# Top-k attention followed by two feed-forward layers on one core: value loads on 128 partitions, last rows of two batches moved to a later stage, DMA issues planned with slack, small operations on GpSimd

## The chip, the cores and the metric

One core of a Trainium2 chip runs the whole program. The metric is the device time of one execution in microseconds (us). The engines are TensorE (PE; its weight loads are shown apart as PEld), VectorE (DVE), ScalarE (ACT), GpSimd (POOL) and SyncE (SP), which here only issues DMA transfers. Each engine takes its instructions in the order in which the program lists them: an instruction that waits holds up everything behind it on its engine.

## What is computed

Attention over 4 batches, 8 heads, 576 rows and head dimension 64, in which each row keeps its 32 largest scores; then two feed-forward layers (512 to 2048 to 512) over all 2304 rows, one with a leaky maximum and one with a clipped square. All in float32.

```python
scores = scale * np.matmul(q, k.transpose(0, 1, 3, 2))
kth = np.partition(scores, -32, axis=-1)[..., -32:-31]
scores = np.where(scores >= kth, scores, -1e9)
scores = scores - scores.max(axis=-1, keepdims=True)
attn = np.exp(scores)
attn = attn / (attn.sum(axis=-1, keepdims=True) + 1e-09)
x = np.matmul(attn, v)                     # heads joined: 2304 rows x 512
h = x @ moe_w_in;   x = np.maximum(0.01 * h, h) @ moe_w_out
h = x @ moe2_w_in;  g = where(h >= 1, h, where(h <= -1, 0, (h + 1) ** 2 / 4))
out = g @ moe2_w_out
```

## The kernel before

The program does not list its instructions in a fixed order. It states operations with an engine, an estimated duration, the tiles that they read and write and a priority (`Plan.op`, L81), and a planner (`Plan.run`, L112) plays them through: each engine takes the ready operation of the lowest priority number. The order in which it starts them is the order in which they are emitted. The constants at the top (`T_NORM`, `HOP`, `LAT`) and the durations given with each operation steer this order; they put no instruction into the program by themselves. A buffer of a tag comes free `HOP` after its last use, and a dependent operation is ready `LAT` after the one it needs (L204 to L220).

Attention is cut into units. A main unit `("m", b, a, h)` takes 256 rows of one head (two tiles of 128 rows). The 64 rows that are left of the 576 in each head are taken by units `("r", b, 0, h)`, one tile for two heads. `units` (L641) lists them by batch; `REMS` (L31) says in which batch's stage the r units of which batches stand: before, those of batches 0 and 1 stand in batch 1's stage, 8 of them, one of each after every second head. An r unit of the batch that is at work uses the K and V that are loaded; an r unit of another batch loads and splits K and V anew (`kv_new`, L473, called at L666).

A unit goes through these steps:
- `kv_new` and `q_new` load K, V and Q with DMAs on SP and split K and Q into a rounded part (ACT) and a rest (POOL, `sub`, L350). For batches 0 and 1 (`lean_of`) V is loaded doubled as `vl`, for batches 2 and 3 as `vraw` and then split into `vv`. V lies in blocks of `KB` = 116 rows, so its loads go to 116 partitions (L482, L486).
- `scores` multiplies on PE into two banks, and ACT copies them to the tile `s`.
- `topk` finds the 32 largest on DVE: four rounds of a maximum of eight (L533) with three replacements (L537) between them. For the first 72 units ACT then makes a mask by a steep slope (L553) and the exponential (L555); their biases are in `nb`, made by a small ACT operation for the unit (L546) and one for each tile (L549). The sums get 1e-9 added on ACT (L568, tile `rc`), DVE takes the reciprocal (L569), POOL scales the rows (L571).
- Two units later `pv` transposes on PE, copies on ACT (`ptr`), for batches 2 and 3 splits into `pt` on ACT and POOL, multiplies by V, and `gather` puts the result into `xraw` (m) or `xr` (r).

When all units of a block of 256 rows are through, `split_x` makes the input of the first feed-forward layer, and `FLOW` (L34) lets the layers run: the two blocks of batch 0 one after the other through layer 0, together through layer 1, then batch 1 through both layers, batch 2, and at last batch 3 together with the block `"r"` of all remaining rows. Feed-forward work has priority numbers from 10000 on: PE takes it where no attention work is ready. The weights are prepared once for each layer (`prep_w`, L402: two ACT and two DVE operations, a split, and a store to scratch memory) while attention of batches 0 and 1 runs; later they are loaded again from scratch into six `ring` buffers.

Of the kernel before, what the change touches and what calls it, by code (L numbers as in the profile page):

```python
# [27 lines left out]
PREP = (0.7, 4.5, 0.05, 14, 14.0, 0.25)  # L28
HOP = 180
JOINT = (1, 2, 3)  # L30
REMS = {1: (0, 1), 2: (2,), 3: (3,)}  # L31
LATE = ("pt", "xb", "vv")
PREPS = ("wraw", "wa", "wb")
FLOW = [  # L34
    ([((0, 0),)], 0),
# [8 lines left out]
]  # L44
LAG = 2
AHEAD = 2
T_NORM = 750
COLD = 100e3
NLEAN = 16
SOFT = (72, 24)  # L50
# [16 lines left out]
class Plan:  # L67
# [44 lines left out]
    def run(self):  # L112
        n = len(self.ops)
        left = [len(o[4]) for o in self.ops]
        succ = [[] for _ in range(n)]
        for i, o in enumerate(self.ops):
            for d in o[4]:
                succ[d].append(i)
        uses = {}
        for o in self.ops:  # L120
            for ref in o[6]:
                uses[ref] = uses.get(ref, 0) + 1
        given = {}
        slots = {t: {i: 0.0 for i in range(c)} for t, c in self.bufs.items()}

        def slot(ref):

            if ref.fifo and given.get(ref.fifo, 0) != ref.seq:
                return None
            free = slots[ref.tag]  # L130
            can = [i for i in (ref.among or free) if free.get(i, 1e18) <= now]
            return min(can, key=free.get) if can else None

        ready_at = [0.0] * n
        ready = {}
        events = []
        busy = {}
        dma_free = 0.0
        order = []
        for i in range(n):  # L140
            if not left[i]:
                ready.setdefault(self.ops[i][0], []).append((self.ops[i][3], i))
        now, cnt = 0.0, 0
        for q in ready.values():
            q.sort()

        def start(i):
            nonlocal dma_free, cnt
            eng, ns, fn, prio, deps, new, refs = self.ops[i]
            for ref in new:  # L150
                ref.slot = slot(ref)
                del slots[ref.tag][ref.slot]
                given[ref.fifo] = given.get(ref.fifo, 0) + 1
            order.append((now, i))
            if eng == "SP":
                busy[eng] = now + 500.0
                t0 = max(now + 1200.0, dma_free)
                dma_free = t0 + ns
                end = dma_free + 900.0
                heapq.heappush(events, (now + 500.0, cnt, -1))  # L160
                cnt += 1
            else:
                if eng == "PE" and now < COLD:
                    ns *= 1.9
                busy[eng] = now + ns
                end = now + ns
                heapq.heappush(events, (end, cnt, -1))
                cnt += 1
            heapq.heappush(events, (end, cnt, i))
            cnt += 1  # L170

        def pick(eng):
            q = ready.get(eng)
            if not q:
                return None
            for k, (prio, i) in enumerate(q):
                ok = ready_at[i] <= now
                if ok:
                    new = self.ops[i][5]
                    ok = all(slot(r) is not None for r in new) and all(  # L180
                        r.slot is not None or r.tag not in self.bufs or r in new for r in self.ops[i][6]
                    )
                if ok:
                    del q[k]
                    return i
            return None

        done = 0
        while done < n:
            for eng in list(ready):  # L190
                while busy.get(eng, 0.0) <= now:
                    i = pick(eng)
                    if i is None:
                        break
                    start(i)
            if not events:
                raise RuntimeError("no instruction can go on")
            now = max(now, events[0][0])
            while events and events[0][0] <= now:
                _, _, i = heapq.heappop(events)  # L200
                if i < 0:
                    continue
                done += 1
                eng = self.ops[i][0]  # L204
                for ref in self.ops[i][6]:
                    uses[ref] -= 1
                    if uses[ref] == 0 and ref.tag in self.bufs:
                        slots[ref.tag][ref.slot] = now + HOP
                        heapq.heappush(events, (now + HOP, cnt, -1))
                        cnt += 1  # L210
                for j in succ[i]:
                    left[j] -= 1
                    e2 = self.ops[j][0]
                    lat = LAT.get((eng, e2), HOP)
                    ready_at[j] = max(ready_at[j], now + lat)
                    if not left[j]:
                        bisect.insort(ready.setdefault(e2, []), (self.ops[j][3], j))
                        if ready_at[j] > now:
                            heapq.heappush(events, (ready_at[j], cnt, -1))
                            cnt += 1  # L220
        self.span, self.order = now, order
        for _, i in order:
            self.ops[i][2]()


LAT = {("PE", "A"): 200, ("PE", "V"): 200, ("A", "PE"): 230, ("A", "V"): 142, ("A", "P"): 160, ("V", "A"): 128,
       ("V", "PE"): 230, ("V", "P"): 155, ("P", "A"): 75, ("P", "V"): 34, ("P", "PE"): 203, ("SP", "SP"): 300,
       ("A", "A"): 140, ("V", "V"): 127, ("P", "P"): 100, ("PE", "PE"): 0}
# [23 lines left out]
def kernel(  # L252
# [111 lines left out]

    idt = fixed([128, 128], F32, "idt")
    half = fixed([128, 1], F32, "half")
    tiny = fixed([128, 1], F32, "tiny")
    gate = fixed([1, 1], F32, "gate")

    def constants():  # L370
# [31 lines left out]
    def prep_w(key, j):  # L402
# [4 lines left out]
        if (L, i, c) not in raws:  # L407
# [7 lines left out]
        va = bank(among=(2, 3)) if L == 0 else new("wa", [128, DM])  # L415
        bits = new("wb", [128, DM], I32)
        n = DM
        act(va, lambda: raw()[:, z * 2 * n:(z + 1) * 2 * n].bitcast(F32)[:, 1::2], t_a(n), [va], [raw], pr,
            scale=2.0 ** -112)
        act(bits, lambda: raw()[:, z * 2 * n:(z + 1) * 2 * n].bitcast(U16)[:, 1::4], t_a(n), [bits], [raw], pr,  # L420
            scale=2.0 ** -13, bias=-0.49994)
        for shift, op in ((3, ALU.logical_shift_left), (-(2 ** 31), ALU.bitwise_and)):
            vec(lambda shift=shift, op=op: nc.vector.scalar_tensor_tensor(
                out=bits(), in0=va().bitcast(I32), scalar=shift, in1=bits(), op0=op, op1=ALU.bitwise_or),
                t_v(n), [bits], [va, bits], pr)
        if key in pinned:
            wt = fixed([128, 2, DM], F32R, f"pin{L}_{f}_{c}")
            pin_t[key] = wt
# [44 lines left out]
    def kv_new(b, h, pr):  # L473
# [5 lines left out]
        sub(lambda: kk()[D:2 * D], lambda: raw()[D:2 * D], lambda: kk()[D:2 * D], S, [kk], [raw, kk], pr)  # L479
        if lean_of(b, h):  # L480
            vt = new("vl", [128, NJ, 2 * D])
            dma(lambda: vt()[0:KB], lambda: vd[b, h], 290, [vt], [], pr)  # L482
            return kk, vt
        vt = new("vv", [128, NJ, 2 * D], F32R)
        vraw = new("vraw", [128, NJ, D])
        dma(lambda: vraw()[0:KB], lambda: vm[b, h], 145, [vraw], [], pr)  # L486
        ve = h % 2
        split(lambda a: vt()[0:KB, :, (ve if a == 0 else 1 - ve) * D:(ve if a == 0 else 1 - ve) * D + D],
              lambda: vraw()[0:KB], NJ * D, vt, [vraw, gate], 0, pr)
# [34 lines left out]
    def topk(tiles, soft, pr):  # L524
# [19 lines left out]
        if soft:  # L544

            P.op("A", 100, lambda: nc.scalar.mul(out=nb()[:, 0:n, 0:2], in_=m()[:, 0:n, 0:32:31], mul=-scale),  # L546
                 w=[nb], r=[(m, (i, r)) for i in range(n) for r in (0, 3)], prio=pr)
            for i in range(n):
                act(lambda i=i: nb()[:, i, 2:3], lambda i=i: m()[:, i, 31:32], 95, [(nb, (i, 2))],  # L549
                    [(m, (i, 3)), nb], pr, func=ACTF.Identity, scale=scale, bias=lambda i=i: nb()[:, i, 0:1])  # L550
            for i in range(n):

                slope(es[i], tiles[i], 670, STEEP, [es[i]], [tiles[i], nb], pr,  # L553
                      scale=scale, bias=lambda i=i: nb()[:, i, 1:2])
                P.op("A", 763, lambda i=i: nc.scalar.activation(  # L555
                    out=es[i](), in_=es[i](), func=ACTF.Exp, bias=nb()[:, i, 2:3], accum_out=sums()[:, i:i + 1]),
                    w=[es[i], (sums, i)], r=[es[i], (nb, (i, 2))], prio=pr)
        else:
            P.op("A", 100, lambda: nc.scalar.mul(out=nb()[:, 0:n, 0], in_=m()[:, 0:n, 0], mul=-scale),
                 w=[nb], r=[(m, (i, 0)) for i in range(n)], prio=pr)  # L560
            for i in range(n):
# [3 lines left out]
                    out=es[i](), in0=tiles[i](), scalar=m()[:, i, 31:32], in1=es[i](),  # L565
                    op0=ALU.is_ge, op1=ALU.mult, accum_out=sums()[:, i:i + 1]),
                    900, [es[i], (sums, i)], [tiles[i], (m, (i, 3)), es[i]], pr)
        act(lambda: rc()[:, 0:n], lambda: sums()[:, 0:n], 95, [rc], [sums, tiny], pr, func=ACTF.Identity, bias=tiny)  # L568
        vec(lambda: nc.vector.reciprocal(out=rc()[:, 0:n], in_=rc()[:, 0:n]), 70, [rc], [rc], pr)  # L569
        for i in range(n):  # L570
            P.op("P", T_NORM, lambda i=i: nc.gpsimd.tensor_scalar(  # L571
# [164 lines left out]
    class Rows:  # L736
# [11 lines left out]
        def hidden(self, i, ws):  # L748
# [21 lines left out]
            else:  # L770
# [1 line left out]
                t = new("t", [128, 512])  # L772
                vec(lambda: nc.vector.tensor_scalar(out=t(), in0=ps(), scalar1=-1.0, scalar2=1.0, op0=ALU.max, op1=ALU.min),  # L773
                    602, [t], [ps], hi)
                act(t, t, 520, [t], [t, half], hi, func=ACTF.Square, scale=0.5, bias=half)
                vec(lambda: nc.vector.tensor_tensor(out=gr(), in0=ps(), in1=t(), op=ALU.max), 602, [gr], [ps, t], hi)
                act(lambda: gt()[:, 0], gr, t_a(512), [(gt, (0, 0))], [gr], hi)
            sub(lambda: gt()[:, 1], gr, lambda: gt()[:, 0], 512, [(gt, (0, 1))], [gr, (gt, (0, 0))], hi)
# [124 lines left out]
def laid_out(inputs):  # L903
# [20 lines left out]
    nj = -(-S // KB)  # L924
    vp = np.zeros((B, H, nj * KB, D), v.dtype)
    vp[:, :, :S] = v
    vm = vp.reshape(B, H, nj, KB, D).transpose(0, 1, 3, 2, 4)
    data.append(("vm", vm))
    data.append(("vd", np.concatenate([vm, vm], axis=4)))
    for n in _INS[3:]:  # L930
# [29 lines left out]
```

## Time and profile before

| | us |
|---|---|
| median of 3 runs | 1308.94 (1304.5 to 1309.97) |
| the profiled execution, its device time | 1310.76 |
| the profiled execution, its span from first to last instruction | 1308.9 |
| PE busy in it | 1187.5 (91%) |
| DVE busy | 918.3 (70%) |
| ACT busy | 904.4 (69%) |
| POOL busy | 704.2 (54%) |
| mean granted TensorE clock | 0.964 of full speed |

The profiled execution's time is 1.9 us over its span, and 1.8 us over the median of the runs. Matmuls are pipelined and their ends are modelled, so a busy PE is not a PE at its peak. A wait for several semaphores is put down to the one that came last by the profile.

### The profile page before, as it was taken

To read this page: it belongs to the slowest core of one execution; us is meant where nothing else is said; L and a number is where in the kernel's file an instruction comes from. 1 tells how busy PE (TensorE), PEld (TensorE's weight loads), DVE (VectorE), ACT (ScalarE), POOL (GpSimd) and SP (SyncE) were. 2 spreads that over 40 slices of the span, in tenths; PEclk is the share of its full clock that TensorE was granted. 3 is DMA by queue.
4 is the path that set the end of the run, shared out by engine and by line. 5 is a ranking of instruction groups with operands and counts; after the bars stand their busy time and mean duration, and the time that the engine had idled before them with its cause. 6 is when DMAs were issued, how large, how long until landed. Compare 5 with 4: busy or idle time off the path is not lost. (4 is left out here: it accounts for less than half of the span.)

```text
span 1308.9 us, 19465 instructions
## 1 busy us (share of the span) xinstructions
PE 1187.5 (91%) x6448; PEld 1003.4 (77%) x6448; DVE 918.3 (70%) x1822; ACT 904.4 (69%) x2171; POOL 704.2 (54%) x684
## 2 busy tenths in 40 slices
PE   1667978797898978999999999999999999999998
PEld 1555867696786766888878888887778888888887
DVE  5899989996999986898899999979932100002221
ACT  3997999986888968898899999987642311132222
POOL 2663766543658644478777777777752322242221
PEclk9877999897999998999999999999999999999999
DMA  7473789665778644154444544333345513342333
GB/s 214 138 244 101 252 300 304 213 218 156 270 254 282 238 157 134 53 171 141 148 152 139 168 143 135 124 130 106 129 162 193 193 64 121 124 158 97 129 129 113
DMA packets 67525, 219.26 MB, mean 168 GB/s; under 512 B 7072, under 2 KB 13152, under 8 KB 63328
## 3 DMA queue, kind: packets, MB, share of 16 engines
q1 hardware_dynamic: 67424, 218.02, 49.6%
q8 instruction: 51, 0.84, 0.3%
q14 instruction: 50, 0.41, 0.1%
HBM read 181.29 MB, written 36.70 MB: 167 GB/s over the span
## 5 line engine op out<-in xcount | busy, mean ns | idle before, releaser
L353 POOL TENSOR_TENSOR gt<-gr,gt 128x512 fp32r<-128x512 f32 x144 | 188.0, 1306 | 296.6 <-ACT gt L337 156.8
L533 DVE MAX8 m<-wk 128x8 f32<-128x576 f32 x432 | 309.7, 747 | 0.8
L726 PE MATMUL bank<-x,ring 128*128 128x512 f32 (+1 forms) x632 | 231.6, 367 | 12.0 <-DMA ring<-scr 7.7
L773 DVE TENSOR_SCALAR t<-bank 128x512 f32<-128x512 f32 x72 | 49.4, 686 | 262.7 <-POOL x L353 142.7
L728 PE MATMUL bank<-x,ring 128*128 128x512 f32 (+1 forms) x632 | 225.7, 357 | 1.6 <-POOL ring L353 1.6
L727 PE MATMUL bank<-x,ring 128*128 128x512 f32 (+1 forms) x632 | 225.6, 357 | 1.2 <-POOL x L353 1.2
L537 DVE MATCH_REPLACE8 wk<-m,wk 128x576 f32<-128x576 f32 x288 | 212.3, 742 | 0.0
L510 PE MATMUL bank<-kk,qh 128*128 128x288 f32 x640 | 139.6, 328 | 51.4 <-ACT qh L337 16.2
L571 POOL TENSOR_SCALAR e<-e,rc 128x576 f32<-128x576 f32 x144 | 108.2, 762 | 115.9 <-DVE rc L569 90.6
L510 PEld LDWEIGHTS bank<-kk,qh 128*128 128x128 f32 x640 | 104.5, 200 | 74.3 <-ACT s L337 22.5
L586 PE MATMUL bank<-idt,e 128*116 128x128 f32 (+1 forms) x720 | 118.4, 292 | 31.0 <-POOL e L571 23.6
L726 PEld LDWEIGHTS bank<-x,ring 128*128 128x128 f32 x632 | 120.8, 191 | 26.3 <-DMA ring<-scr 8.6
L353 POOL TENSOR_TENSOR pt<-ptr,pt 116x512 fp32r<-116x512 f32 (+1 forms) x112 | 121.8, 1107 | 33.7 <-ACT pt L337 21.9
L728 PEld LDWEIGHTS bank<-x,ring 128*128 128x128 f32 x632 | 120.5, 191 | 19.7 <-POOL ring L353 2.0
L726 PE MATMUL bank<-gt,ring 128*128 128x256 f32 (+1 forms) x384 | 133.0, 346 | 1.0 <-ACT ring L337 1.0
L339 ACT ACTIVATE t<-t,half 128x512 f32<-128x512 f32 x72 | 52.2, 725 | 118.0 <-DVE t L773 117.9
L586 PEld LDWEIGHTS bank<-idt,e 128*116 128x116 f32 (+1 forms) x720 | 87.4, 142 | 59.9 <-POOL e L571 33.5
L728 PE MATMUL bank<-gt,ring 128*128 128x256 f32 (+1 forms) x384 | 130.5, 340 | 2.1 <-POOL ring L353 2.1
L727 PEld LDWEIGHTS bank<-x,ring 128*128 128x128 f32 x632 | 120.9, 191 | 14.5 <-POOL x L353 2.6
L727 PE MATMUL bank<-gt,ring 128*128 128x256 f32 (+1 forms) x384 | 129.6, 338 | 0.0
L337 ACT COPY ptr<-bank 116x512 f32<-116x512 f32 (+1 forms) x224 | 106.8, 514 | 26.2 <-PE bank L586 25.1
L610 PE MATMUL bank<-ptr,vl 116*128 116x256 f32 (+3 forms) x480 | 111.9, 387 | 13.7 <-ACT ptr L337 13.5
(72 smaller groups left out, 2698.3 us busy)
## 6 DMA issues: line engine op xcount, KB each, us to landing
ring<-scr SPq DMA_DIRECT2D x212, 512.0 KB
scr<-ring SPq DMA_DIRECT2D x61, 512.0 KB
wraw<-in_moe_w_in_dram SPq DMA_DIRECT2D x16, 1024.0 KB
wraw<-in_moe_w_out_dram SPq DMA_DIRECT2D x16, 1024.0 KB
kraw<-in_km_dram SPq DMA_DIRECT2D x48, 288.0 KB
vl<-in_vd_dram SPq DMA_DIRECT2D x32, 290.0 KB
qraw<-in_qm_dram SPq DMA_DIRECT2D x24, 256.0 KB
out_dram<-t SPq DMA_DIRECT2D x16, 256.0 KB
```

The source lines that it names most:

```text
L337: nc.scalar.copy(out=out_(), in_=in_())
L339: nc.scalar.activation(out=out_(), in_=in_(), func=func, **a)
L353: lambda: nc.gpsimd.tensor_tensor(out=out_(), in0=in0(), in1=in1(), op=ALU.subtract),
L510: nc.tensor.matmul(ps()[:, 0:HALF], lhsT=qh()[:, part, t * 128:(t + 1) * 128], rhs=kk()[:, c * HALF:(c + 1) * HALF], start=(i == 0), stop= ...
L533: vec(lambda i=i, c=c, src=src: nc.vector.max(out=m()[:, i, c], in_=src()), 664, [(m, (i, r))], [src], pr)
L537: vec(lambda i=i, c=c, src=src, w=ws[i]: nc.vector.match_replace(out=w(), in_to_replace=m()[:, i, c], in_values=src(), imm_value=NEG), 720 ...
L571: P.op("P", T_NORM, lambda i=i: nc.gpsimd.tensor_scalar(out=es[i](), in0=es[i](), scalar1=rc()[:, i:i + 1], scalar2=1.0, op0=ALU.mult, op1 ...
L586: nc.tensor.transpose(ps()[0:p, i * 128:(i + 1) * 128], e()[:, cols[j]], idt())
L610: nc.tensor.matmul(out_ps()[:, c0:c1], lhsT=vt()[0:p, j, :], rhs=pt()[0:p, c] if lean else pt()[0:p, part, c], start=bi == 0 and part == 0 ...
L726: nc.tensor.matmul(ps, lhsT=wh, rhs=xh, start=first, stop=False, skip_group_check=True)
L727: nc.tensor.matmul(ps, lhsT=wh, rhs=xl, start=False, stop=False, skip_group_check=True)
L728: nc.tensor.matmul(ps, lhsT=wl, rhs=xh, start=False, stop=last, skip_group_check=True)
```

## The change

- The host lays V out with 128 partitions for each block (12 rows of zeros behind the 116), and the loads of `vl` and `vraw` fill all 128 partitions: 320 and 160 KB in place of 290 and 145. The computation reads 116 as before.
- `REMS` puts the r units of batches 0 and 1 into batch 2's stage: 12 r units there, none in batch 1's.
- The planner counts 2.5 us (`SLACK`) more before a DMA issue that depends on another engine's operation, and before a buffer that a load fills counts as free.
- The exponential's second bias is a difference on POOL, one for each unit, in place of one ACT operation for each tile; 1e-9 is added on POOL in place of ACT.
- Some estimated durations of the planner are changed (`T_NORM`, the weights' preparation, the square of layer 1).

```diff
-REMS = {1: (0, 1), 2: (2,), 3: (3,)}
+REMS = {2: (0, 1, 2), 3: (3,)}
+LOADED = ("kraw", "vraw", "qraw", "vl", "wraw")
-T_NORM = 750
+T_NORM = 720
...
                     if uses[ref] == 0 and ref.tag in self.bufs:
-                        slots[ref.tag][ref.slot] = now + HOP
-                        heapq.heappush(events, (now + HOP, cnt, -1))
+                        hop = HOP + (SLACK if ref.tag in LOADED else 0.0)
+                        slots[ref.tag][ref.slot] = now + hop
+                        heapq.heappush(events, (now + hop, cnt, -1))
...
-                    lat = LAT.get((eng, e2), HOP)
+                    lat = LAT.get((eng, e2), HOP) + (SLACK if e2 == "SP" and eng != "SP" else 0.0)
...
+SLACK = 2500.0
...
-    tiny = fixed([128, 1], F32, "tiny")
+    tiny = fixed([128, 2], F32, "tiny")
...
-        act(va, lambda: raw()[:, z * 2 * n:(z + 1) * 2 * n].bitcast(F32)[:, 1::2], t_a(n), [va], [raw], pr,
+        act(va, lambda: raw()[:, z * 2 * n:(z + 1) * 2 * n].bitcast(F32)[:, 1::2], 560, [va], [raw], pr,
...
-                t_v(n), [bits], [va, bits], pr)
+                t_v(n) if L == 0 else 805, [bits], [va, bits], pr)
...
-            dma(lambda: vt()[0:KB], lambda: vd[b, h], 290, [vt], [], pr)
+            dma(vt, lambda: vd[b, h], 320, [vt], [], pr)
...
-        dma(lambda: vraw()[0:KB], lambda: vm[b, h], 145, [vraw], [], pr)
+        dma(vraw, lambda: vm[b, h], 160, [vraw], [], pr)
...
             P.op("A", 100, lambda: nc.scalar.mul(out=nb()[:, 0:n, 0:2], in_=m()[:, 0:n, 0:32:31], mul=-scale),
-                 w=[nb], r=[(m, (i, r)) for i in range(n) for r in (0, 3)], prio=pr)
+                 w=[(nb, 0)], r=[(m, (i, r)) for i in range(n) for r in (0, 3)], prio=pr)
+            P.op("P", 180, lambda: nc.gpsimd.tensor_tensor(
+                out=nb()[:, 0:n, 2], in0=nb()[:, 0:n, 0], in1=nb()[:, 0:n, 1], op=ALU.subtract),
+                w=[(nb, 2)], r=[(nb, 0)], prio=pr)
             for i in range(n):
-                act(lambda i=i: nb()[:, i, 2:3], lambda i=i: m()[:, i, 31:32], 95, [(nb, (i, 2))],
-                    [(m, (i, 3)), nb], pr, func=ACTF.Identity, scale=scale, bias=lambda i=i: nb()[:, i, 0:1])
...
-        act(lambda: rc()[:, 0:n], lambda: sums()[:, 0:n], 95, [rc], [sums, tiny], pr, func=ACTF.Identity, bias=tiny)
+        P.op("P", 180, lambda: nc.gpsimd.tensor_tensor(
+            out=rc()[:, 0:n], in0=sums()[:, 0:n], in1=tiny()[:, 0:n], op=ALU.add), w=[rc], r=[sums, tiny], prio=pr)
...
-                act(t, t, 520, [t], [t, half], hi, func=ACTF.Square, scale=0.5, bias=half)
+                act(t, t, 620, [t], [t, half], hi, func=ACTF.Square, scale=0.5, bias=half)
...
-    vm = vp.reshape(B, H, nj, KB, D).transpose(0, 1, 3, 2, 4)
+    vm = np.zeros((B, H, 128, nj, D), v.dtype)
+    vm[:, :, :KB] = vp.reshape(B, H, nj, KB, D).transpose(0, 1, 3, 2, 4)
```

## Rows read from the trace of the kernel before

**Rows 1.** Stages: us, busy (instructions) by engine, granted clock, DMA share, GB/s

```profile
25.00:250.00 225.00, 165.38 (x921) 141.85 (x921) 209.14 (x427) 197.00 (x479) 126.77 (x124) 0.88 0.66 220
250.00:525.00 275.00, 244.23 (x1354) 207.55 (x1355) 247.61 (x470) 221.12 (x527) 153.01 (x136) 0.93 0.64 216
525.00:955.00 430.00, 423.61 (x2341) 351.77 (x2340) 396.32 (x825) 379.65 (x977) 317.79 (x328) 1.00 0.41 135
955.00:1308.90 353.90, 349.08 (x1819) 298.23 (x1818) 52.03 (x77) 94.69 (x169) 99.67 (x88) 1.00 0.39 134
```

**Rows 2.** DVE's groups, 0 to 525: xcount | busy us, mean ns | idle before

```profile
L533 DVE MAX8 m<-wk 128x8 f32<-128x576 f32 x216 | 154.4, 745 | 0.0
L537 DVE MATCH_REPLACE8 wk<-m,wk 128x576 f32<-128x576 f32 x144 | 106.0, 741 | 0.0
...
L533 DVE MAX8 m<-s 128x8 f32<-128x576 f32 x74 | 53.0, 744 | 4.7 <-ACT s L337 4.7
L537 DVE MATCH_REPLACE8 wk<-m,s 128x576 f32<-128x576 f32 x72 | 53.0, 740 | 0.0
```

**Rows 3.** DVE's waits (us, times, longest): 25 to 525, 25 to 40, 300 to 320, 490 to 500

```profile
DVE rc L569 <- ACT rc L339: 33.7, 8, 9.8
...
DVE rc L569 <- ACT rc L339: 8.5, 1, 8.5
...
DVE rc L569 <- ACT rc L339: 9.8, 1, 9.8
...
DVE rc L569 <- ACT rc L339: 8.9, 1, 8.9
```

**Rows 4.** Stretches 12 to 20 (with its V loads issued) and 150 to 175, as rows 1

```profile
12.00:20.00 8.00, 3.47 (x10) 2.54 (x11) 5.30 (x11) 5.93 (x13) 5.33 (x5) 1.00 0.26 100
...
vl<-in_vd_dram SPq DMA_DIRECT2D x1, 290.0 KB
vraw<-in_vm_dram SPq DMA_DIRECT2D x2, 145.0 KB
...
150.00:175.00 25.00, 19.33 (x117) 16.67 (x116) 22.80 (x46) 24.00 (x56) 17.71 (x16) 0.90 0.99 353
```

**Rows 5.** Waits for a DMA: 25 to 40, 300 to 320, 474 to 498, 25 to 525

```profile
ACT wb L339 <- DMA wraw<-in_moe_w_in_dram: 10.9, 1, 10.9
...
PE bank L726 <- DMA ring<-scr: 7.7, 2, 4.2
...
ACT vv L337 <- DMA vraw<-in_vm_dram: 9.6, 2, 7.6
...
ACT kk L337 <- DMA kraw<-in_km_dram: 1.3, 1, 1.3
```

**Rows 6.** ACT in order of time (start, us): the last part of batch 1's input

```profile
527.31 0.39 ACT L337 CAST x<-xraw 128x256 fp32r<-128x256 f32 x1
```

**Rows 7.** PE's groups, 525 to 955, of the forms of an r unit

```profile
L510 PE MATMUL bank<-kk,qh 128*128 128x288 f32 x304 | 64.8, 311 | 1.6 <-ACT ptr L337 0.7 <-ACT s L337 0.3 <-ACT xraw L337 0.2
...
L586 PE MATMUL bank<-idt,e 128*116 128x128 f32 x292 | 40.8, 274 | 2.7 <-ACT s L337 1.7 <-ACT xb L337 0.6 <-POOL e L571 0.4
...
L610 PE MATMUL bank<-ptr,vl 116*128 116x64 f32 x32 | 3.8, 271 | 0.0
```

**Rows 8.** Groups of the whole span that bear on ACT's and POOL's small operations

```profile
L353 POOL TENSOR_TENSOR gt<-gr,gt 128x512 fp32r<-128x512 f32 x144 | 188.0, 1306 | 296.6 <-ACT gt L337 156.8 <-ACT gr L339 135.3 <-issue 1.9
...
L339 ACT ACTIVATE e<-s,nb 128x576 f32<-128x576 f32 x144 | 106.8, 773 | 0.5
...
L353 POOL TENSOR_TENSOR kk<-kraw,kk 64x576 fp32r<-64x576 f32 x48 | 68.9, 1441 | 34.8 <-ACT nb L546 14.9 <-ACT kk L337 9.3 <-issue 6.6
...
L339 ACT ACTIVATE nb<-m,nb 128x1 f32<-128x1 f32 x130 | 35.1, 297 | 1.1
...
L339 ACT ACTIVATE rc<-sums,tiny 128x2 f32<-128x2 f32 x64 | 19.3, 302 | 0.8 <-DVE e L564 0.6
...
L695 POOL TENSOR_TENSOR xr<-xr,xb 128x64 f32<-128x64 f32 x8 | 2.6, 323 | 5.7 <-ACT xb L337 5.6
```

More of the change, by code (lines that the diff above doesn't have):

```diff
@@ L417, in prep_w @@
         n = DM
-        act(va, lambda: raw()[:, z * 2 * n:(z + 1) * 2 * n].bitcast(F32)[:, 1::2], t_a(n), [va], [raw], pr,
+        act(va, lambda: raw()[:, z * 2 * n:(z + 1) * 2 * n].bitcast(F32)[:, 1::2], 560, [va], [raw], pr,
             scale=2.0 ** -112)
-        act(bits, lambda: raw()[:, z * 2 * n:(z + 1) * 2 * n].bitcast(U16)[:, 1::4], t_a(n), [bits], [raw], pr,
+        act(bits, lambda: raw()[:, z * 2 * n:(z + 1) * 2 * n].bitcast(U16)[:, 1::4], 560, [bits], [raw], pr,
             scale=2.0 ** -13, bias=-0.49994)
@@ L546, in topk @@
             P.op("A", 100, lambda: nc.scalar.mul(out=nb()[:, 0:n, 0:2], in_=m()[:, 0:n, 0:32:31], mul=-scale),
-                 w=[nb], r=[(m, (i, r)) for i in range(n) for r in (0, 3)], prio=pr)
+                 w=[(nb, 0)], r=[(m, (i, r)) for i in range(n) for r in (0, 3)], prio=pr)
+            P.op("P", 180, lambda: nc.gpsimd.tensor_tensor(
+                out=nb()[:, 0:n, 2], in0=nb()[:, 0:n, 0], in1=nb()[:, 0:n, 1], op=ALU.subtract),
+                w=[(nb, 2)], r=[(nb, 0)], prio=pr)
             for i in range(n):
-                act(lambda i=i: nb()[:, i, 2:3], lambda i=i: m()[:, i, 31:32], 95, [(nb, (i, 2))],
-                    [(m, (i, 3)), nb], pr, func=ACTF.Identity, scale=scale, bias=lambda i=i: nb()[:, i, 0:1])
-            for i in range(n):
-                slope(es[i], tiles[i], 670, STEEP, [es[i]], [tiles[i], nb], pr,
+                slope(es[i], tiles[i], 670, STEEP, [es[i]], [tiles[i], (nb, 0)], pr,
                       scale=scale, bias=lambda i=i: nb()[:, i, 1:2])
@@ L556, in topk @@
                     out=es[i](), in_=es[i](), func=ACTF.Exp, bias=nb()[:, i, 2:3], accum_out=sums()[:, i:i + 1]),
-                    w=[es[i], (sums, i)], r=[es[i], (nb, (i, 2))], prio=pr)
+                    w=[es[i], (sums, i)], r=[es[i], (nb, 2)], prio=pr)
         else:
```

## The prediction, made before the changed kernel ran

> **What bounds the kernel now.** I read the stages first, then who waits in each, then the DMA. [rows 1] cuts the span at the moments where batch 0 is through (about 250 us), where batch 1's last block reaches the first feed-forward layer (527 us, [rows 6]) and where the last attention work ends (955 us). From 525 us on, PE is idle for 430 - 423.6 = 6.4 us and then for 353.9 - 349.1 = 4.8 us, at a granted clock of 1.00: with attention of the next batch and a stock of feed-forward work it always has something to do, and it alone sets the end. Before 525 us it is starved: 225 - 165.4 = 60 us idle from 25 to 250 us and 275 - 244.2 = 31 us from 250 to 525 us, at clocks of 0.88 and 0.93. In those two stages DVE is busy for 209 of 225 and 248 of 275 us, so the top-k search and the weights' preparation on DVE set the pace there. Of what DVE does not use, 33.7 us lie in eight waits of the reciprocal for ACT, and three of these are long: 8.5, 9.8 and 8.9 us [rows 3].
>
> The three long ones look alike: everything stands still until a DMA lands. Near 30 us ACT waits 10.9 us for a weight load; near 300 to 320 us PE waits 7.7 us for two ring loads; between 474 and 498 us ACT waits 9.6 us for two V loads [rows 5]. In the stretch of 12 to 20 us, when V loads were being issued, the 16 DMA engines are busy to 0.26, which is 4 of 16, and move 100 GB/s; at 150 to 175 us, with loads of 128 partitions, they reach 0.99 and 353 GB/s [rows 4]. So a V load of 116 partitions runs on four engines, and whatever is queued behind it on these four comes late, although twelve are idle.
>
> So the end is: the moment when batch 1 is ready (call it D, now 527 us) plus PE's work after it. What moves D moves the end, less what PE work is shifted behind D.
>
> **The change part by part.** The sum is made against the profiled execution: 1310.8 us, of which 1308.9 is its span and 1.9 lies around it; the median of the runs is 1.8 us lower, and I subtract that at the end.
>
> *Padding V.* A V load of 297 KB at 100 GB/s takes 3 us on its four engines; 328 KB at 353 GB/s takes 0.9 us. At each of the three long waits several V loads stand in a row, and the wait should shrink to what is late next. Gone at most: 8.5 + 9.8 + 8.9 = 27 us of DVE time before D. I take 22, leaving some 2 us at each place for the next late thing. Lower bound 0 (the loads stay on four engines), upper 27. The 10% more bytes cost nothing where DMA is at 0.66 or less [rows 1].
>
> The Trainium skill (DMA: Bandwidth & Descriptors, section on why a DMA increments its semaphore by 16) says that a transfer uses the largest number of engines up to 16 that divides its outer dimension: 4 for 116 and 16 for 128. By that rule the whole 22 us come; were engines handed out by bytes instead, none would. The 0.26 of [rows 4] agrees with it.
>
> *Moving the r units.* Batch 1's stage loses 8 r units, each one tile. A tile costs DVE four maxima and three replacements: by busy time over count 154.4/216 = 0.715, 53.0/74 = 0.716, 106.0/144 and 53.0/72 = 0.736 us, so 4 x 0.715 + 3 x 0.736 = 5.1 us, and 8 tiles 41 us before D [rows 2]. Since DVE sets the pace there, D comes 41 us earlier, if PE can follow. It can: the stage of 250 to 525 us shrinks by 41 us and by two of the three holes (some 15 us) to about 219 us. PE was busy for 244 us in it and loses the r units' 29 us (below), which leaves 215; at a clock of 1.00 instead of 0.93 these are about 200, or 91%. That is tight, and I take 3 us off. The r units' PE work now stands behind D. One has 8 score matmuls, 5 transposes and 10 products: by busy over count [rows 7] 8 x 0.213 + 5 x 0.140 + 10 x 0.12 = 3.6 us, 29 us for eight. Busy time overlaps in a pipeline, so this is an upper end; I take 25 and 20 as the lower end.
>
> What else is moved: the r units' Q loads and, since batch 1's heads are no longer at hand, 8 more K and 8 more V loads with 8 more K splits in batch 2's stage: on POOL 8 x 1.44 = 12 us [rows 8], on ACT some 8 x 0.7, on the DMA queue some 5 MB. POOL is busy for 318 of 430 us there, DMA to 0.41 [rows 1], and attention in that stage has room to be late: PE lives on feed-forward work in stock. At 955 us there are still 354 us of it, of which the last group (batch 3 and the r rows, three of nine blocks) needs about 270, so attention may end some 80 us later than now before PE notices. Cost taken: 0.
>
> *Small operations to POOL.* ACT loses 130 operations of 35.1 us and 80 of some 24 us in all [rows 8], about 59 us. Before D ACT is not the bound (197 of 225, 221 of 275 us), so I count nothing; at most 6 us of DVE's short waits (33.7 - 27.2) could go. POOL gets 72 + 80 = 152 operations on one or two columns. The trace has none so small; the nearest is 0.32 us at 64 columns, two inputs [rows 8]. From below, nothing under 0.1 us stands to reason; I take 0.2 us, 30 us spread over the span, on an engine with room. What counts is the new wait. The second bias is needed by the exponential on ACT, behind which the evictions of scores and transposes are queued, for which PE waits; the mask operation of 0.77 us [rows 8] stands between and covers a free POOL. The sum is needed by DVE's reciprocal, behind which the next tile's maxima are queued. If POOL is in a split of 1.3 us [rows 8], the wait is up to 1.3 us. Bounds over the 32 units before D: 0 to 32 x 1.3 = 42 us of DVE time. I take 0, since the order is planned with these operations on POOL, and keep the other end.
>
> *Slack and estimates.* They add no instruction and change the order. K loads are waited for once in 25 to 525 us, 1.3 us [rows 5], so 2.5 us later is covered in nearly all cases; where it isn't (batch 0's 16 units have the shortest lead), 16 x 2.5 = 40 us is the far end. A gain is as possible, from an SP that stands less before a buffer that is not yet free, up to the waits for DMA left over, some 5 us. I take 0.
>
> *Sum.* D moves by 22 + 41 - 3 = 60 us, to about 467 us; PE has 25 us more behind it: 60 - 25 = 35 us. 1310.8 - 35 = 1275.8, less 1.8: 1274 us.
>
> **The rivals.**
> 1. *The move only displaces.* Between 250 us and D the chain of weight preparation and layers of batch 0 holds PE back as much as DVE does, or PE runs dry behind D because three r units in a row need six K tiles where five buffers exist. Then the 41 us and the 25 us cancel, and the padding's 22 us are left: 1310.8 - 22 - 1.8 = 1287 us. For it: PE at 91% has no precedent before D (it had 244/275 = 89% there). Against: the tiles' 41 us are plain DVE time.
> 2. *Padding does nothing*: the holes stay, 35 - 22 = 13 us: 1296 us. Against: 0.26 and 100 GB/s in [rows 4].
> 3. *Slower: POOL becomes a link of the chain.* Each unit's exponential and reciprocal wait for a POOL that is in its splits. It decides where the loss before D passes the gain: 60 - 25 = 35 us over 32 units, 1.1 us for each in the mean, nearly a whole split before every unit. At two splits, 2 x 1.3 x 32 = 83 us, D falls behind where it was, and the time is 1310.8 + 83 - 35 - 1.8, about 1357; at 1.5 us a unit it is 1322. For it: POOL at 56% before D. Against: the mask operation covers half of it, and a small operation at 0.2 us is ready to go ahead of a split.
> 4. *A new order, new holes.* A planner's order that changes everywhere opens other waits of the size of the old ones, some 35 us in all: 1303 to 1314 us.
> 5. *More of all*: 27 + 41 + 6 - 20 = 54 us: 1255 us.
>
> **How the numbers follow.** A difference under 0.5% (1302.4 to 1315.5 us) is about what a measurement of this kernel cannot tell from no change. Chances: forecast (1260 to 1283) 0.53; rival 1 (to 1292) 0.15; rival 2 (to 1302) 0.08; rival 5 (below 1260) 0.09; rival 4 0.08; rival 3 0.07. Faster 0.53 + 0.15 + 0.08 + 0.09 = 0.85, same 0.08, slower 0.07. The range from 1250 to 1302 leaves out rivals 3 and 4 and the far end of 5.
>
> **What would show it.** In the new profile: in a stretch with V loads the DMA share is well over 0.26; none of the three waits of 8 us is left; the last input cast of batch 1 starts near 467 us; PE's idle time behind it stays near 1.5%. Wrong would be: waits of the exponential or the reciprocal for POOL that add up to tens of us (rival 3), PE gaps between D and the end (rival 1), attention that ends later than some 80 us before the last group can (then the move costs).

## The result

| | before | after |
|---|---|---|
| median of the runs, us | 1308.87 | 1257.23 (1256.8 to 1258.68) |
| ratio, 95% interval | | 0.9613 (0.959 to 0.9637) |
| profiled span, us | 1308.9 | 1256.9 |
| last input cast of batch 0, us | 241.0 | 222.8 |
| last input cast of batch 1 (D), us | 527.3 | 459.0 |
| from D to the end, us | 781.6 | 797.9 |

The medians are of four runs each. The change saves 51.6 us; 35 were forecast (1274 us, range 1250 to 1302). The time lies inside the range, but under the band that the forecast was given (1260 to 1283), in that of rival 5, which had a chance of 0.09. D came 68 us earlier (60 forecast), and the stretch behind D became 16 us longer (25 forecast).

The stages of the changed kernel, cut at batch 0's last cast, at D and where the last attention work ends (us, then busy time and instructions of PE, PEld, DVE, ACT, POOL, granted clock, DMA share, GB/s):

```profile
25.00:222.80 197.80, 155.78 (x870) 133.91 (x871) 193.59 (x398) 173.91 (x395) 127.09 (x149) 0.88 0.67 232
222.80:459.00 236.20, 215.95 (x1211) 184.59 (x1209) 229.37 (x433) 195.45 (x423) 140.97 (x150) 0.99 0.69 237
459.00:925.60 466.60, 464.57 (x2639) 393.86 (x2640) 423.94 (x893) 401.62 (x970) 374.56 (x455) 1.00 0.46 156
925.60:1256.90 331.30, 326.44 (x1717) 280.42 (x1715) 46.92 (x68) 87.43 (x155) 88.79 (x78) 1.00 0.38 131
```

[rows 1] cuts the kernel before at 250 us, 9 us behind its cast of batch 0. Cut at the two casts, its first two stages are:

```profile
25.00:241.00 216.00, 158.93 (x875) 136.24 (x875) 200.84 (x410) 188.53 (x457) 121.14 (x118) 0.87 0.67 224
241.00:527.30 286.30, 252.79 (x1412) 214.83 (x1410) 257.04 (x490) 230.85 (x554) 158.64 (x141) 0.93 0.63 211
```

Behind D PE idles for 2.0 and 4.9 us: it is the bound there as before. Between batch 0 and D it idles for 20 us instead of 34, at a clock of 0.99 instead of 0.93, and DVE is busy for 229 of 236 us: it sets the pace with almost no hole left. The first stage is still starved (42 us idle instead of 57, clock 0.88). The two casts that mark the cuts, ACT in order of time:

```profile
222.83 0.39 ACT L340 CAST x<-xraw 128x256 fp32r<-128x256 f32 x1
...
459.00 0.39 ACT L340 CAST x<-xraw 128x256 fp32r<-128x256 f32 x1
```

DVE's waits from 25 to 460 us of the changed kernel (us, times, longest), against [rows 3]:

```profile
DVE rc L573 <- POOL rc L571: 4.5, 5, 2.0
DVE wb L426 <- ACT wb L342: 2.6, 4, 1.6
DVE wb L426 <- ACT bank L342: 2.2, 5, 0.8
```

The 33.7 us in waits of the reciprocal are 4.5, and none is longer than 2 us. In the stretch of 12 to 20 us, where [rows 4] had four engines at work:

```profile
12.00:20.00 8.00, 2.66 (x8) 1.99 (x8) 7.96 (x19) 5.38 (x12) 2.38 (x3) 1.00 1.04 406
```

The DMA share is 1.04 instead of 0.26. V loads still move in it, though not alone: by their size, 434 of its 1055 packets are rows of `vl` and `vraw` (2560 and 1280 bytes), 205 of 310 in the kernel before. They have been issued before this stretch begins: SP in order of time (start, us), first the kernel before, then the changed one.

```profile
11.57 0.70 SPq L331 DMA_DIRECT2D vl<-in_vd_dram  x1
12.31 4.84 SPq L331 DMA_DIRECT2D vraw<-in_vm_dram  x2
17.27 3.04 SPq L331 DMA_DIRECT2D wraw<-in_moe_w_in_dram  x1
```

```profile
6.45 1.21 SPq L334 DMA_DIRECT2D vl<-in_vd_dram  x2
7.71 0.93 SPq L334 DMA_DIRECT2D vraw<-in_vm_dram  x2
10.73 0.33 SPq L334 DMA_DIRECT2D wraw<-in_moe_w_in_dram  x1
```

Before, SP spent 4.84 us on the issue of two loads and 3.04 us on a weight load; after, 0.93 and 0.33 us. Not only what was queued came late, the issue itself stood.

### The profile page after: what moved, and what is told of

Same layout as the page of the kernel before. It is cut to its first block, busy times and chain, and to the rows that moved or that the text cites. A ratio compares the mean times of both kernels' runs of the same rounds, so it can differ in the third digit from the quotient of the medians.

```text
span 1256.9 us, 19365 instructions
## 1 busy us (share of the span) xinstructions
PE 1168.0 (93%) x6448; PEld 996.8 (79%) x6448; DVE 910.3 (72%) x1822; ACT 873.7 (70%) x1969; POOL 740.0 (59%) x844
## 4 chain that ended last, share of the span: by engine, by line
PE 63%; ACT 4%; DVE 3%; POOL 2%; issue 2%; DMA 1%; POOLq 0%; ACTq 0%; DVEq 0%
PE bank L730 12%; PE bank L731 12%; PE bank L732 12%; PE bank L614 6%; PE bank L801 5%; PE bank L802 4%; PE bank L803 4%; PE bank L513 4%; PE bank L590 4%; DVE wb L426 1%; POOL ring L356 1%; ACT e L558 1%; DMA scr<-ring 1%; ACT e L342 1%; DVE m L536 0%
## 5 line engine op out<-in xcount | busy, mean ns | idle before, releaser
L730 PE MATMUL bank<-x,ring 128*128 128x512 f32 (+1 forms) x632 | 228.6, 362 | 3.0 <-DVE gr L780 1.5
L513 PE MATMUL bank<-kk,qh 128*128 128x288 f32 x640 | 135.5, 322 | 45.0 <-ACT s L340 13.8
L732 PEld LDWEIGHTS bank<-x,ring 128*128 128x128 f32 x632 | 119.2, 189 | 20.0 <-POOL ring L356 2.5
L730 PEld LDWEIGHTS bank<-x,ring 128*128 128x128 f32 x632 | 119.6, 189 | 16.5 <-DVE gr L780 2.4
L731 PEld LDWEIGHTS bank<-x,ring 128*128 128x128 f32 x632 | 119.6, 189 | 13.2 <-POOL x L356 1.5
L340 ACT COPY s<-bank 128x288 f32<-128x288 f32 x288 | 107.7, 405 | 22.9 <-PE bank L513 21.5
```

Source lines behind the costliest of these rows:

```text
L340: nc.scalar.copy(out=out_(), in_=in_())
L513: nc.tensor.matmul(ps()[:, 0:HALF], lhsT=qh()[:, part, t * 128:(t + 1) * 128], rhs=kk()[:, c * HALF:(c + 1) * HALF], start=(i == 0), stop= ...
L730: nc.tensor.matmul(ps, lhsT=wh, rhs=xh, start=first, stop=False, skip_group_check=True)
L731: nc.tensor.matmul(ps, lhsT=wh, rhs=xl, start=False, stop=False, skip_group_check=True)
L732: nc.tensor.matmul(ps, lhsT=wl, rhs=xh, start=False, stop=last, skip_group_check=True)
```

## The experiments

Twelve kernels: each of four parts alone on the kernel before, each taken out of the changed kernel (and the planner's estimates, the fifth part), and three that part order from work. The estimates were taken out but not put in alone. Times are medians; differences are against the kernel before, which was timed again beside each group of kernels (1308.4 to 1309.9 us), or the changed kernel (1257.2 us), which was not timed again. The table gives the three stretches of the profiled execution's span for the kernel before, the changed one and nine of the twelve, each cut at the same two casts. That execution is within 2 us of the median, with slack alone 4.7 us under it:

| kernel | to batch 0's cast | from there to D | D to the end | median |
|---|---|---|---|---|
| before | 241.0 | 286.3 | 781.6 | 1308.9 |
| padding alone | 228.6 | 266.0 | 782.9 | 1279.3 |
| moved r units alone | 243.5 | 239.5 | 814.5 | 1299.0 |
| small operations alone | 239.2 | 275.7 | 777.3 | 1292.8 |
| slack alone | 241.0 | 266.8 | 778.2 | 1292.5 |
| changed kernel | 222.8 | 236.2 | 797.9 | 1257.2 |
| without padding, same order | 232.8 | 239.3 | 797.9 | 1271.2 |
| without the move | 226.5 | 269.7 | 778.4 | 1276.1 |
| without the small operations | 229.6 | 233.7 | 805.5 | 1272.6 |
| the same order, small operations on ACT | 226.2 | 244.8 | 810.2 | 1284.8 |
| without slack | 225.2 | 238.6 | 803.8 | 1269.7 |

### Padding alone, every engine in the order of before

```diff
-            dma(lambda: vt()[0:KB], lambda: vd[b, h], 290, [vt], [], pr)
+            dma(vt, lambda: vd[b, h], 290, [vt], [], pr)
-        dma(lambda: vraw()[0:KB], lambda: vm[b, h], 145, [vraw], [], pr)
+        dma(vraw, lambda: vm[b, h], 145, [vraw], [], pr)
...
+    vm = np.zeros((B, H, 128, nj, D), v.dtype)
+    vm[:, :, :KB] = vp.reshape(B, H, nj, KB, D).transpose(0, 1, 3, 2, 4)
```

> The kernel before with V padded to 128 partitions and nothing else; the planner keeps the old costs of these loads, so every engine has the order of before. Theory (V loads on four of the 16 DMA engines make the three long holes): the waits of 8.5, 9.8 and 8.9 us are gone, DMA share in a stretch of V loads well over 0.26, and the time falls by 22 to 35 us, to 1274 to 1287 us. Rival (the holes come from the place of the loads in SP's order, and the padding only moves more bytes): 1305 to 1312 us.

Measured: 1279.29 us, ratio 0.9771 (0.975 to 0.9792), 30.6 us less than the kernel before in the same order. The stretch of 12 to 20 us, columns as above:

```profile
12.00:20.00 8.00, 2.66 (x8) 1.99 (x8) 7.96 (x19) 5.86 (x13) 2.44 (x4) 1.00 1.05 413
```

DVE's wait for the sums from ACT, from 25 us to D, first in the kernel before, then in this one:

```profile
DVE rc L569 <- ACT rc L339: 34.8, 9, 9.8
...
DVE rc L569 <- ACT rc L339: 6.8, 8, 2.3
```

The three long waits of [rows 3] are gone (34.8 us became 6.8, the longest 2.3), and since no instruction changed its place, the four-engine V loads made them. The rival is out. The granted clock between batch 0 and D rose with it, from 0.93 to 0.97; no run parts what came by the clock from what came by the waits.

### The moved r units alone

```diff
-REMS = {1: (0, 1), 2: (2,), 3: (3,)}
+REMS = {2: (0, 1, 2), 3: (3,)}
```

> The kernel before with the r units of batches 0 and 1 in batch 2's stage and nothing else (V loads on 116 partitions). Theory (41 us of DVE time leave the time before D, 25 us of PE time come behind it, holes stay): 1285 to 1298 us. Rival (the move only displaces): 1302 to 1315 us; if the four-engine loads, which now come in one stage, open larger holes there, slower still.

Measured: 1299.04 us, ratio 0.9925 (0.9905 to 0.9945), 10.9 us less. D comes 44 us earlier, and the way from D to the end is 33 us longer: both halves of the step are there, with a time 1 us above the interval named (1285 to 1298).

### The small operations alone

```diff
-                act(lambda i=i: nb()[:, i, 2:3], lambda i=i: m()[:, i, 31:32], 95, [(nb, (i, 2))],
+            P.op("P", 180, lambda: nc.gpsimd.tensor_tensor(
+                out=nb()[:, 0:n, 2], in0=nb()[:, 0:n, 0], in1=nb()[:, 0:n, 1], op=ALU.subtract),
...
-        act(lambda: rc()[:, 0:n], lambda: sums()[:, 0:n], 95, [rc], [sums, tiny], pr, func=ACTF.Identity, bias=tiny)
+        P.op("P", 180, lambda: nc.gpsimd.tensor_tensor(
+            out=rc()[:, 0:n], in0=sums()[:, 0:n], in1=tiny()[:, 0:n], op=ALU.add), w=[rc], r=[sums, tiny], prio=pr)
```

> The kernel before with the two small operations on POOL and nothing else. Prediction's step: no effect, 1300 to 1315 us. Rival (POOL as a link of the chain): waits of the reciprocal and the exponential for POOL of 30 us and more before D, and 1320 us or more. Second rival (the gain beyond the forecast is ACT's relief): 1285 to 1295 us.

Measured: 1292.75 us, ratio 0.9875 (0.9853 to 0.9898), 17.2 us less, the second rival's number. In the trace 10.6 us of it lie between batch 0 and D, 4.3 behind D. The planner made a new order here, so this kernel does not part ACT's relief from the order; a later one does.

### The slack alone

```diff
+SLACK = 2500.0
+                        hop = HOP + (SLACK if ref.tag in LOADED else 0.0)
...
+                    lat = LAT.get((eng, e2), HOP) + (SLACK if e2 == "SP" and eng != "SP" else 0.0)
```

> The kernel before planned with 2.5 us slack for DMA issues and freed load buffers, nothing else. Prediction's step: no effect beyond a new order, 1300 to 1315 us. Rival (the gain beyond the forecast comes from an SP that stands less): 1285 to 1297 us, and the holes at 30 us and 300 us smaller though V loads stay on four engines.

Measured: 1292.51 us, ratio 0.987 (0.9838 to 0.9903), 17.4 us less. DVE's waits from 25 to 508 us, and those from 300 to 320 us:

```profile
DVE rc L572 <- ACT rc L342: 19.7, 13, 9.2
...
DVE rc L572 <- ACT rc L342: 2.8, 2, 2.1
```

The hole at the start stands (9.2 us, against what the rival expected), that of 300 to 320 us went from 9.8 to 2.8 us, and the one near 490 us is gone, with V still on four engines. A new order of the same transfers is enough for that. So part of what the slack gives alone is what the padding gives too.

### Without the padding, every engine in the order of the changed kernel

```diff
-            dma(vt, lambda: vd[b, h], 320, [vt], [], pr)
+            dma(lambda: vt()[0:KB], lambda: vd[b, h], 320, [vt], [], pr)
-        dma(vraw, lambda: vm[b, h], 160, [vraw], [], pr)
+        dma(lambda: vraw()[0:KB], lambda: vm[b, h], 160, [vraw], [], pr)
...
-    vm = np.zeros((B, H, 128, nj, D), v.dtype)
-    vm[:, :, :KB] = vp.reshape(B, H, nj, KB, D).transpose(0, 1, 3, 2, 4)
+    vm = vp.reshape(B, H, nj, KB, D).transpose(0, 1, 3, 2, 4)
```

> The changed kernel with V loads on 116 partitions again; the planner keeps the costs of 320 and 160 KB, so every engine has the order of the changed kernel. Theory (the padding does its work whatever the order): the hole at 30 us is back, the first reciprocal at 38 us instead of 26 us, and later holes where V loads stand in a row, in all 15 to 35 us: 1272 to 1292 us. Rival (slack and the new order already keep the loads out of the way, as the kernel before with slack alone lost its holes at 300 and 490 us): only the hole at the start returns, 1266 to 1272 us.

Measured: 1271.21 us, 14.0 us more; the rival. The stretch of 12 to 20 us:

```profile
12.00:20.00 8.00, 3.54 (x10) 2.61 (x11) 5.36 (x11) 5.85 (x13) 5.33 (x5) 1.00 0.26 101
```

Two of its waits from 25 to 472 us, ACT's and DVE's:

```profile
ACT wb L342 <- DMA wraw<-in_moe_w_in_dram: 11.0, 1, 11.0
...
DVE rc L573 <- POOL rc L571: 13.2, 8, 8.4
```

The four engines and the hole at the start are back, batch 0's cast is 10 us later and the next stretch 3 us longer; behind D not a microsecond differs. In the changed kernel's order the padding is worth little beyond the start. In the order of before it was worth 31 us, because there V loads also stood in front of ring loads near 300 us (SP issued four V loads from 290 to 295 us and ring loads at 297) and of each other near 480 us.

### Without the move

```diff
-REMS = {2: (0, 1, 2), 3: (3,)}
+REMS = {1: (0, 1), 2: (2,), 3: (3,)}
```

> The changed kernel with the r units of batches 0 and 1 in batch 1's stage again. Theory (41 us of DVE time before D against 25 us of PE work behind it, 16 us net by the prediction, 11 us when done alone): D near 500 us, 1265 to 1273 us. Rival (with the holes gone PE is the bound before D too, so the move is worth nothing): 1254 to 1261 us.

Measured: 1276.12 us, 18.9 us more. D is 37 us later, and the stretch behind D 19.5 us shorter. The theory holds, 3 us above the interval named; PE is not yet the bound before D.

### Without the small operations

```diff
-            P.op("P", 180, lambda: nc.gpsimd.tensor_tensor(
-                out=nb()[:, 0:n, 2], in0=nb()[:, 0:n, 0], in1=nb()[:, 0:n, 1], op=ALU.subtract),
...
+                act(lambda i=i: nb()[:, i, 2:3], lambda i=i: m()[:, i, 31:32], 95, [(nb, (i, 2))],
```

> The changed kernel with both small operations on ACT again. Done alone the step gave 17 us, most of it as shorter holes before D. Theory (those were the holes of the V loads, which the padding removes anyway): within 6 us of the changed kernel, 1252 to 1264 us. Rival (ACT's relief of 59 us of busy time lets PE's attention work through faster, before D and behind it): 1268 to 1275 us.

Measured: 1272.56 us, 15.3 us more. The theory that only holes of the V loads were filled falls: with V padded the step is worth nearly as much. In the trace 6.8 us are lost before batch 0's cast, 2.5 come back before D, and 7.6 us are lost behind D. DVE's waits from 463 to 942 us:

```profile
DVE m L536 <- ACT s L340: 22.7, 7, 10.0
DVE rc L572 <- ACT rc L342: 16.4, 17, 3.1
```

The maxima wait 22.7 us for score copies that come late on ACT (in the changed kernel 7.6 us in the whole span). DVE has room behind D, so this wait alone is not the price; and since the order is new too, the next kernel holds it.

### The small operations back on ACT, in the order planned for POOL

```diff
-            P.op("P", 180, lambda: nc.gpsimd.tensor_tensor(
-                out=nb()[:, 0:n, 2], in0=nb()[:, 0:n, 0], in1=nb()[:, 0:n, 1], op=ALU.subtract),
+            P.op("P", 180, lambda: [nc.scalar.activation(
+                out=nb()[:, i, 2:3], in_=nb()[:, i, 1:2], func=ACTF.Identity, scale=-1.0, bias=nb()[:, i, 0:1])
+                for i in range(n)], w=[(nb, 2)], r=[(nb, 0)], prio=pr)
...
+        P.op("P", 180, lambda: nc.scalar.activation(
+            out=rc()[:, 0:n], in_=sums()[:, 0:n], func=ACTF.Identity, bias=tiny()[:, 0:1]),
```

> The changed kernel in its own order (the planner still plans the small operations as 180 ns on POOL), but at these points ACT makes them: one operation for each tile for the second bias, one for each unit for the 1e-9, as before the change. It parts the relief of ACT from the new order. Theory A (ACT's relief is what gave 15 us: ACT now has some 200 operations of 0.3 us more, 59 us, and its copies of scores and transposes come later): 1268 to 1280 us. Theory B (the gain was the order that the planner found with the operations on POOL): 1254 to 1262 us.

Measured: 1284.81 us, 27.6 us more, above theory A's interval and far from theory B's. All other work has the same place on its engine, so what is lost comes from ACT making these operations. D is 12.0 us later. DVE's wait for the sums from 25 us to D (4.5 us in the changed kernel):

```profile
DVE rc L574 <- ACT rc L571: 14.5, 20, 2.6
```

That is 10.0 us more, most of the 12.0: the small operation for the sums now stands in ACT's queue, and the reciprocal waits for it 20 times instead of 5. The stretch from D to the end, in the first fence of the changed kernel, in the second of this one:

```profile
459.00:1256.90 797.90, 791.01 (x4354) 674.29 (x4354) 470.86 (x961) 489.06 (x1124) 463.35 (x533) 1.00 0.43 145
```

```profile
471.00:1281.20 810.20, 798.95 (x4354) 672.94 (x4354) 471.61 (x959) 507.99 (x1236) 448.90 (x446) 1.00 0.42 143
```

The same 4354 matmuls at the same clock take 12.3 us longer, and ACT is busy for 19 us more. PE is idle for 4.4 us more, in which its waits for copies on ACT grow from 1.9 to 5.5 us. The other 8 us lie within PE's busy time; through what, stays open. That the planner, told of ACT's work, loses only 15.3 us (the kernel before this one) shows that its order recovers some 12.

### Without slack, with other slacks, with the old estimates

```diff
-SLACK = 2500.0
+SLACK = 1250.0
...
-T_NORM = 720
+T_NORM = 750
```

Of the four kernels one has the first edit, one the same with 4000.0, one has all lines of the slack taken out, and one has the second edit with the old durations of the preparation and the square.

> The changed kernel planned without the slack. Done alone the step gave 17 us, and its holes at 317 and 498 us were gone. Theory (the same holes again, which the padding removes anyway): within 6 us of the changed kernel, 1252 to 1264 us. Rival (SP that stands before a buffer delays loads whatever the engines): 1268 to 1276 us, with waits for K, Q or ring loads.

> The changed kernel with a slack of 1.25 us instead of 2.5 us. Slack of 0 gave 1269.7 us. Theory A (the slack works by its size: SP stands less before buffers that are not free yet): between the two, 1260 to 1266 us. Theory B (only the order that comes out counts): anywhere from 1254 to 1275 us, not between the two by more than chance.

> The changed kernel with a slack of 4 us instead of 2.5 us. Theory A (the slack works by its size and 2.5 us already covers the lateness): 1254 to 1260 us. Theory B (only the order that comes out counts): anywhere from 1254 to 1275 us.

> The changed kernel planned with the old estimates (norm 750, weight preparation and square by the formulas). No instruction is added or taken away, only the order changes. It measures what a change of order alone can do once the holes of the V loads are gone. Theory A (with the holes gone, orders differ little): 1254 to 1261 us. Theory B (any new order moves the time by 10 us and more, so the 15 us of the small operations and the 12 us of the slack may be that): 1265 to 1275 us.

Measured: without slack 1269.71 us (12.5 more), with 1.25 us 1257.89 us, with 4 us 1260.0 us, with the old estimates 1261.68 us (4.5 more). All four differ from the changed kernel in order alone. Three lie within 5 us of it, and one, without slack, does not: that order costs 12.5 us. The slack does not work by its size, since 1.25 us give all that 2.5 us give; theory A for 1.25 us (1260 to 1266) is out, and 4 us fit both theories. The old estimates come out 0.7 us above their theory A. The time without slack is its rival's (1268 to 1276 us), but of the waits that it named ring loads hold PE for 2.7 us in all and a K load ACT for 0.9 us.

In the trace without slack 5.9 us are lost behind D and 4.8 before. Before D DVE does not wait more: from the start to D it idles for 16.5 us instead of 19.6. One group of its operations is longer, the second half of the weights' preparation, first in the changed kernel up to D, then without slack:

```profile
L426 DVE SCALAR_TENSOR_TENSOR wb<-wa,wb 128x512 int32<-128x512 int32 x64 | 58.0, 926 | 2.4 <-ACT wb L342 2.1 <-ACT wa L342 0.2
...
L423 DVE SCALAR_TENSOR_TENSOR wb<-wa,wb 128x512 int32<-128x512 int32 x64 | 65.8, 1046 | 0.6 <-ACT wb L339 0.5
```

The same 64 operations are busy for 7.8 us more. By start and end times in the trace without slack, 14 of them with next to no two-input operation on POOL beside them took 0.69 us in the mean, and 41 with one beside them for over 0.4 us took 1.25 us. So what this order loses before D can lie in what it puts side by side, not in a wait for a load; no run tests that. What is lost behind D stays open.

## Why the prediction was right, and where its sizes were off

**What bounds** held: the time is D plus what PE has behind D. In the changed kernel these are 459.0 and 797.9 us. With padding alone D came 32.7 us earlier, the stretch behind it stayed within 1.3 us, and the span lost 31.4. It did not hold that PE alone sets the stretch behind D: with the same 4354 matmuls it took 797.9 to 810.2 us.

**Padding.** The mechanism was right (a DMA share of 0.26, three holes), the size was not: 22 us taken, 30.6 measured alone. I counted the 8.5 us of DVE near 38 us and left out the wait of 4.7 us for the first scores, which stands in [rows 2]; the Q load that these scores need stands behind a V load too (ACT's cast of it waits 3.25 us). DVE's first scores and its first reciprocal, in the kernel before and with padding alone:

```profile
14.66 0.76 DVE L533 MAX8 m<-s 128x8 f32<-128x576 f32 x1 [4.67 <-ACT s L337]
38.61 0.17 DVE L569 RECIPROCAL rc<-rc 128x2 f32<-128x2 f32 x1 [8.53 <-ACT rc L339]
```

```profile
11.32 0.76 DVE L533 MAX8 m<-s 128x8 f32<-128x576 f32 x1 [1.34 <-ACT s L337]
26.65 0.16 DVE L569 RECIPROCAL rc<-rc 128x2 f32<-128x2 f32 x1
```

The first reciprocal came 12.0 us earlier, 3.3 of them by the first scores. The next late thing, for which I kept some 2 us at each hole, cost nothing: 27.2 + 3.3 us make 30.5, against 30.6 measured. In the changed kernel the 22 us did not come as forecast: there the padding is worth 14.0, 10 of them at the start, since the two later holes do not come back without it. The DMA share of 0.26 with 116 partitions is about 4/16, and with 128 it is 1.05 in the same stretch of the same order. By the rule of the Trainium skill (DMA: Bandwidth & Descriptors, section on why a DMA increments its semaphore by 16) a transfer on 116 partitions takes 4 engines and one on 128 takes 16. The trace agrees.

**The move.** 41 - 25 = 16 us were taken; alone it gave 10.9, taken out of the changed kernel 18.9. D moved by 44 and 37 us, the stretch behind D by 33 and 19.5 us. So the step stands: 38 us of D (41 less 3) and 25 behind it were taken, between what the two kernels show; how much of PE's work finds a gap behind D depends on the rest.

**Small operations: the step that failed.** Taken as 0 because ACT "is not the bound"; worth 15 to 17 us, and 28 us where the order is held. The relief itself was over-counted: 59 us by the sum of the groups, but ACT's operations overlap, and its busy time fell by 36 us with this step alone (904 to 869). The price of the operation was right, 0.2 us taken against these groups of the changed kernel (busy us, mean ns):

```profile
L571 POOL TENSOR_TENSOR rc<-sums,tiny 128x2 f32<-128x2 f32 x64 | 12.9, 202 | 74.6 <-ACT e L558 72.2 <-DVE e L567 2.1
L551 POOL TENSOR_TENSOR nb<-nb 128x2 f32<-128x2 f32 x58 | 11.7, 201 | 29.7 <-ACT nb L549 28.7 <-DMA wraw<-in_moe_w_in_dram 0.4
```

The feared link (rival 3) is not there; the changed kernel's waits for POOL's two results in the whole span:

```profile
ACT e L558 <- POOL nb L551: 3.0, 5, 1.0
...
DVE rc L573 <- POOL rc L571: 31.0, 22, 9.5
```

Only 4.5 of the 31 us lie before D, where DVE counts. What I overlooked is that before the change the sums were already a link of the chain, on ACT: an operation of 0.3 us there stands in order behind ACT's copies, and ACT is busy to 88% in the first stage. With the order held, DVE waits for the sums for 14.5 us before D if ACT makes them and for 4.5 if POOL does; behind D, PE's waits for ACT's copies grow. I had priced ACT's own idle time, not the lateness of what it passes on.

**Slack.** Taken as 0; worth 17.4 us alone and 12.5 us in the changed kernel. I had allowed for some 5 us of gain. Alone, part of it was two of the V loads' holes. The 12.5 us are an order's, and only a part of them is traced (above).

**The sum.** Alone the four parts give 30.6 + 10.9 + 17.2 + 17.4 = 76 us, together (with the estimates' 4.5) 52: padding and slack in part fill the same holes. But taken out they cost 14.0 + 18.9 + 15.3 + 12.5 + 4.5 = 65 us, also more than 52, so overlap is not the whole of it; new orders move the time by some us too. The forecast's 35 us missed 17: 8 us in D (18 us instead of some 7 up to batch 0's cast, 50 instead of 53 from there) and 9 us behind D. Of the 11 missed up to batch 0's cast some 3 are the padding's start (10 in this order). The kernels without the small operations and without slack lose 6.8 and 2.4 us before batch 0's cast and 7.6 and 5.9 us behind D; that these are the rest of the 17 is an argument by size and place. So it is partly luck that D came within 8 us of its forecast: the padding gave less in this order than was taken, and two parts taken as 0 gave something. Rival 5's sum of 54 us came nearest, with 27 us for the padding, 6 for the small operations and none for the slack: its total was right, its terms were not.

**Rivals.** 1 (only displaced) is out: without the move the kernel takes 18.9 us more, and PE's idle time between batch 0 and D fell. 2 is out by the padding alone. 4 (new holes) is out: no wait of DVE between 25 and 460 us is over 2 us.

## What to carry to other kernels

Here loads of 116 partitions kept the DMA share at 0.26 and made what was queued behind them late; look for stretches with a share near 4/16 and for long waits on transfers that are themselves well shaped, and try padding. An engine below 90% that hands tiles to the bound engine in order is not free: price the lateness of what it passes on, not its idle time. Parts of one change do not add up, so measure each both alone and taken out, and hold the order where the planner would change it.

## What the runs showed of the hardware that was not expected

The issue of a DMA on SP itself took 2.3 and 2.5 us for two V loads and 3.0 us for the weight load behind them while the DMA share stood at 0.26; the median of all issues is 0.33 us, and the longest in the changed kernel is 1.4 us. A GpSimd operation with two inputs on one or two columns takes 0.20 us, less than ACT's 0.30 us for the same columns. The DMA share reached 1.05 at 413 GB/s in a stretch in which padded V, weight, K and Q loads stood in a row. The same operation of the weights' preparation on DVE took 0.69 us with next to no two-input operation on POOL beside it and 1.25 us beside one (without slack).
